# Cutting the first weight load in two and reordering the loads and scans of the second pair in a fused scan and feed-forward kernel

## Chip, core and metric

The kernel runs on one core of a Trainium2 chip. The metric is device time in microseconds (us), as the median over runs. An execution that was also profiled gives the trace; its own time and its span, from the first to the last profiled instruction, are given below.

## What is computed

A chunked state-space layer is followed by a bilinear feed-forward layer. Batch is 4, heads 8, sequence 768, head width 32, state width 16; the feed-forward layer goes from 256 to 1536 and back.

```python
# per chunk: decay L from a, intra-chunk part, carried state
M = einsum('bhin,bhjn->bhij', Cc, Bc) * L          # causal
y = einsum('bhij,bhjd->bhid', M, xc) + einsum('bhin,bhnd->bhid', Cc, state) * decay_to_i
state = decay_full * state + sum_j(B x decay)
# then, on tokens x (3072, 256)
out = ((x @ w_a) * (x @ w_b)) @ w_out
```

All inputs and the output are float32.

## The kernel before

The sequence is cut into six blocks of 128 positions. A *pair* is one block of two of the four batches, so there are twelve pairs; pairs 0 and 1 are block 0. The instruction order on each engine is written out by hand (`manual_schedule`), so what stands earlier in the program is issued earlier on its engine. Engines meet through semaphores alone.

What happens to a pair: its inputs B (`bn`), C (`cn`) and x (`xn`) are loaded in two halves each, one batch a half (`load1(queue, pair, which, bt)`, line L138, `which` being 0 for B, 1 for C and 2 for x). B and C are scaled by decay factors (`scale_bc`, L271, results `bm` and `cm`). TensorE transposes both (`transposes`, L293); ScalarE (L304) and VectorE (L305) copy the transposes out as `bt` and `ct`. TensorE makes the scores (`scores`, L327); they are masked in four pieces, three by VectorE (L361) and one by ScalarE and GpSimd (`by_pool`, copy L358 and product L359, tile `t`). x is scaled to f16 by ScalarE (`scale_x`, L255, tile `x`). Then TensorE forms the output (`pv`, `pv_u`, L370) and the state's summand (`ds_mm`, L387), and the result is copied out to `X2T` (L419, L420; for pair 0 L475 and L477). From there the feed-forward products start: `unit_mm` (L528) makes two of the twelve 128-column groups of `x @ w_a` (`aps`) or `x @ w_b` (`bps`); ScalarE copies `aps` out (L542), VectorE multiplies (L549), and `out_mm` (L564) makes the output.

The decay factors come from six scans on VectorE (`scan(lo, hi)`, L208), one a block, each from `a_sb` and a tile of zeros. `over_mid` (L211) and `sel_over_mid` (L214) prepare the factor products `fps` (L229).

The weights are float32 in memory and f16 on the chip, so they are loaded from GpSimd's queue, which converts them: `load_w(half)` (L146) loads half the columns of `w_a` and then of `w_b`, 128 x 2 x 768 elements each. GpSimd's loads go through one queue (q0) and are moved in the order of their issue. GpSimd issues, in its own instruction stream, B and C of pair 1, the first half of the weights, both halves of x of pair 1, and then computes the masked product of pair 0 and the scaled B of pair 1.

TensorE is kept busy while it would wait by products of zeros whose results nobody reads (`warmup(n, bank, cols)`, L201). Ahead of the first feed-forward products stand two of them (L710).

```python
    transposes(1, apart=True)
    scan(5, NBLK)
    over_mid(1, NBLK)
    sel_over_mid(1, NBLK, nc.vector)
    warmup(2, tcp)
    aps = [unit_mm(0, 0, Wa), unit_mm(0, 1, Wa)]
    asb = [evac_a(aps[0])]
    scores(1)
```

Later in the program the first load on SyncE's queue for pair 3 waits for the second half of `w_b` to land.

Of the kernel before, what the change touches and what calls it, by code (L numbers as in the profile page):

```python
# [10 lines left out]
f16 = mybir.dt.float16  # L11
# [16 lines left out]
def kernel(  # L28
# [13 lines left out]
    nc = tc.nc  # L42
# [4 lines left out]
    NBLK = S // Q  # L47
# [34 lines left out]
    big = ctx.enter_context(tc.tile_pool(name="big", bufs=1))  # L82
    a_sb = big.tile([BH, NBLK, Q], f32, name="a_sb")
    zero = big.tile([BH, Q], f32, name="zero")
    KC = d_ff // 2
    Wa = [big.tile([128, 2, KC], f16, name=f"Wa{t}") for t in range(2)]
    Wb = [big.tile([128, 2, KC], f16, name=f"Wb{t}") for t in range(2)]
    Wo = big.tile([128, NK, d_model], f16, name="Wo")
    X2T = big.tile([128, P0, 2, 2, Q], f16, name="X2T")
# [35 lines left out]
    def bank(name):  # L125
        return psf.tile([128, 512], f32, name=name, tag=f"ff{next(banks)}")
# [8 lines left out]
    def load1(eng, p, which, bt, i0=0, n=64):  # L135
        blk, bp = divmod(p, NBP)
        src = (B, C, x)[which][2 * bp + bt, :, blk * Q + 2 * i0 : blk * Q + 2 * i0 + 2 * n, :]
        return eng.dma_start(  # L138
            pair_in[p][which][64 * bt + i0 : 64 * bt + i0 + n].rearrange("i h r n -> i h (r n)"),
            src.rearrange("h (i r) n -> i h (r n)", r=2),  # L140
        )

    def load_w(half):
        c = slice(half * KC, (half + 1) * KC)
        return [
            nc.gpsimd.dma_start(W[half], src.rearrange("(f p) e -> p f e", p=128)[:, :, c])  # L146
            for W, src in ((Wa, moe_w_a), (Wb, moe_w_b))
        ]

    def load_wo(half):  # L150
        nc.gpsimd.dma_start(
# [35 lines left out]
    for bt in range(2):  # L187
        v = causal[64 * bt : 64 * bt + 64]
# [3 lines left out]
    load1(nc.gpsimd, 1, 0, 1)  # L192
    load1(nc.gpsimd, 1, 1, 0)
    load1(nc.gpsimd, 1, 1, 1)
    load_w(0)
    for bt in range(2):
        load1(nc.gpsimd, 1, 2, bt)

    def warmup(n, bank, cols=512):
        for _ in range(n):  # L200
            nc.tensor.matmul(  # L201
                bank[:, 0:cols], warm[:, 0:128], warm[:, 0:cols], start=True, stop=True, skip_group_check=True
            )


    def scan(lo, hi):
        for k in range(lo, hi):
            nc.vector.tensor_tensor_scan(Pr[:, k], a_sb[:, k], zero, 1.0, ALU.mult, ALU.add)  # L208
# [12 lines left out]
    def factors_mm(lo, hi, fps=None, k0=0):  # L221
        if fps is None:
            fps = bank("fps")
        w = 2 * NBP * H
        F = fps[:, k0 * w : (k0 + hi - lo) * w].rearrange("p (k r c) -> p k r c", k=hi - lo, r=2)
        for k in range(lo, hi):
            for r in range(2):
                for bt in range(2):
                    nc.tensor.matmul(  # L229
                        F[64 * bt : 64 * bt + 64, k - lo, r],  # L230
                        Pr[:, k].rearrange("p (i r) -> p r i", r=2)[:, r],
                        selr[:, k, bt],
                        start=True,
                        stop=True,
                        skip_group_check=True,
                        tile_position=(0, 64 * bt),
                    )
        return F.rearrange("p k r c -> p (k r c)")
# [5 lines left out]
    def flat(f, lo, hi):  # L244
        return f[:, lo:hi].rearrange("p k r b h -> p (k r b h)")
# [13 lines left out]
    def scale_bc(p, which, eng, factor=None):  # L259
        blk, bp = divmod(p, NBP)  # L260
        name, f = (("bm", fB), ("cm", fC))[which]
        if p >= P0 and which:
            eng.tensor_tensor(
                out=planes[p % 2][:, 4:6].rearrange("p r (h n) -> p r h n", n=N),
                in0=pair_in[p][which].rearrange("p h r n -> p r h n"),
                in1=f[:, blk, :, bp].unsqueeze(3).broadcast_to((128, 2, H, N)),
                op=ALU.mult,
            )
            return
        m_ = mid.tile([128, 2, H, N], f16, name=name, tag=name)  # L270
        eng.tensor_tensor(  # L271
            out=m_,
            in0=pair_in[p][which].rearrange("p h r n -> p r h n"),
            in1=(f[:, blk, :, bp] if factor is None else factor).unsqueeze(3).broadcast_to((128, 2, H, N)),
            op=ALU.mult,
        )
        st.setdefault(p, {})[name] = m_
        if p >= P0:
            dst = planes[p % 2][:, 0:4].rearrange("p (r e) (m f n) -> p r e m f n", e=2, f=2, n=N)
            for e in range(2):  # L280
                eng.tensor_copy(dst[:, :, e, :, e], m_.rearrange("p r (m f) n -> p r m f n", f=2)[:, :, :, e])
# [81 lines left out]
    def pv_u(p, u, py, first):  # L363
        s = st[p]
        for r in range(2):
            for g in range(4):
                for bt in range(2):
                    h = u * 4 + g
                    k = slice(64 * bt, 64 * bt + 64)
                    nc.tensor.matmul(  # L370
                        py[bt, u][32 * (g ^ 2 * bt) : 32 * (g ^ 2 * bt) + 32] if p >= P0 else py[bt][32 * g : 32 * g + 32, u * Q : (u + 1) * Q],
                        s["X16"][k, h, r, :],
                        s["T1"][k, h, r, :],
                        start=(first and u == 0 and r == 0),
                        stop=(r == 1),
                        skip_group_check=True,
                        tile_position=(64 * bt, 32 * (g ^ 2 * bt) if p >= P0 else 32 * g),
                    )
# [93 lines left out]
    def evac0(u, bt, eng, py):  # L472
        o_, i_ = X2T[:, 0, bt, u], py[bt][:, u * Q : (u + 1) * Q]
        if eng is nc.scalar:
            nc.scalar.activation(out=o_, in_=i_, func=AF.Copy, scale=YS / XS)  # L475
        else:
            nc.vector.tensor_scalar(o_, i_, YS / XS, None, ALU.mult)  # L477
# [45 lines left out]
    def unit_mm(p, k2, W):  # L523
        ps = bank("aps" if W is Wa else "bps")
        for kk in range(2):
            k = 2 * k2 + kk
            for f in range(2):
                nc.tensor.matmul(  # L528
                    ps[:, kk * 2 * Q : (kk + 1) * 2 * Q],
                    W[k // 6][:, f, k % 6 // 3 * 384 : (k % 6 // 3 + 1) * 384].rearrange("p (c kk) -> p kk c", kk=3)[  # L530
                        :, k % 3
                    ],
                    X2T[:, p, :, f],
                    start=(f == 0),
                    stop=(f == 1),
                    skip_group_check=True,
                )
        return ps

    def evac_a(a_ps, on_dve=False):  # L540
        asb = ffh.tile([128, 512], f32, name="asb", tag="asb")
        (nc.vector.tensor_copy if on_dve else nc.scalar.copy)(asb, a_ps)  # L542
        return asb
# [42 lines left out]
    def bunit(blk, k):  # L586
        s = st.setdefault(("FF", blk), {})
        if "hk" not in s:
            s["hk"] = hkb.tile([128, NK, 2 * NBP * Q], f16, name="hkb", tag="hkb")
        ps = []  # L590
        for W in (Wa, Wb):
            t_ = bank("aps" if W is Wa else "bps")
            for f in range(2):
                nc.tensor.matmul(  # L594
                    t_,
                    W[k // 6][:, f, k % 6 // 3 * 384 : (k % 6 // 3 + 1) * 384].rearrange("p (c kk) -> p kk c", kk=3)[
                        :, k % 3
                    ],
                    XB[:, blk - P0 // NBP, f].rearrange("p t j q -> p (t j q)"),
                    start=(f == 0),  # L600
                    stop=(f == 1),
                    skip_group_check=True,
                )
            ps.append(t_)
        asb = evac_a(ps[0])
        return lambda: nc.vector.tensor_tensor(out=s["hk"][:, k], in0=ps[1], in1=asb, op=ALU.mult)  # L606
# [64 lines left out]
    v = factors_mm(0, 1)  # L671
# [2 lines left out]
    warmup(1, SC[3], 128)  # L674
    scale_bc(0, 0, nc.vector)
    scale_bc(0, 1, nc.vector, v.rearrange("p (r b h) -> p r b h", r=2, b=NBP)[:, :, 0])
    tb, tcp = bank("tb"), bank("tc")
    transposes(0, [tb, tcp], lambda: warmup(1, SC[3], 128))
    nc.scalar.copy(flat(fC, 0, 1), v)
    scan(3, 4)  # L680
    warmup(1, SC[3])
    warmup(2, SC[3], 128)
    scores(0)
# [4 lines left out]
    mask(product0(1, 0))  # L688
    warmup(5, tcp)
    scale_bc(1, 1, nc.vector)  # L690
    scale_bc(1, 0, nc.gpsimd)
    py = [bank("py0"), bank("py1")]
    pv_u(0, 0, py, True)
    for bt in range(2):
# [3 lines left out]
    pv_u(0, 1, py, True)  # L698
    for bt in range(2):
        evac0(1, bt, (nc.scalar, nc.vector)[bt], py)  # L700
    scan(4, 5)
    w1 = load_w(1)
    for bt in range(2):
        load1(nc.gpsimd, 2, 0, bt)
    warmup(1, tcp, 128)
    transposes(1, apart=True)
    scan(5, NBLK)
    over_mid(1, NBLK)
    sel_over_mid(1, NBLK, nc.vector)
    warmup(2, tcp)  # L710
    aps = [unit_mm(0, 0, Wa), unit_mm(0, 1, Wa)]
    asb = [evac_a(aps[0])]
    scores(1)
# [267 lines left out]
```

## Time and profile before

| What | Value |
|---|---|
| median of 5 runs | 125.78 us (125.61 to 126.6) |
| the profiled execution's own time | 125.61 us |
| its span | 123.9 us |
| TensorE (PE) busy | 118.8 us, 96% of the span |
| VectorE (DVE) busy | 85.4 us, 69% |
| ScalarE (ACT) busy | 72.0 us, 58% |
| GpSimd (POOL) busy | 65.8 us, 53% |
| granted TensorE clock | full in all 40 slices |
| HBM read, written | 11.13 MB, 3.15 MB |

PEld is TensorE's weight load, which runs beside its products. SP is SyncE. In the profile the time from the start of the span stands first in a timeline or a chain, then the duration, both in us; a bracket at the end of a line tells how long the engine stood idle before it and what ended that. "us to landing" counts from a load's issue until its data is there. A line such as `bps<-X2T,Wb` names the tile written and the tiles read. The lines L... are those of the kernel before. Ends of TensorE's products are modelled, and spans on POOL are rough.

### The profile page before, as it was taken

To read this page: it belongs to the slowest core of one execution; us is meant where nothing else is said; L and a number is where in the kernel's file an instruction comes from. 1 tells how busy PE (TensorE), PEld (TensorE's weight loads), DVE (VectorE), ACT (ScalarE), POOL (GpSimd) and SP (SyncE) were. 2 spreads that over 40 slices of the span, in tenths; PEclk is the share of its full clock that TensorE was granted. 3 is DMA by queue.
4 is the path that set the end of the run, shared out by engine and by line. 5 is a ranking of instruction groups with operands and counts; after the bars stand their busy time and mean duration, and the time that the engine had idled before them with its cause. 6 is when DMAs were issued, how large, how long until landed. Compare 5 with 4: busy or idle time off the path is not lost.

```text
span 123.9 us, 4408 instructions
## 1 busy us (share of the span) xinstructions
PE 118.8 (96%) x1775; PEld 81.5 (66%) x1775; DVE 85.4 (69%) x162; ACT 72.0 (58%) x142; POOL 65.8 (53%) x112
## 2 busy tenths in 40 slices
PE   5889999999999999999999999999999999999990
PEld 2436789978898888744467465757464775555890
DVE  1786896795967678498964989748889544747200
ACT  0466755766364785887548746474637746657220
POOL 7999996999987497099930868039400000000000
PEclk9999999999999999999999999999999999999999
DMA  3999999997689569988364351658431023010132
GB/s 65 168 166 233 170 214 155 196 161 145 89 208 135 84 176 109 154 147 222 59 119 98 85 84 32 105 104 153 108 70 42 0 47 85 1 24 19 27 106 85
DMA packets 41844, 13.78 MB, mean 111 GB/s; under 512 B 36592, under 2 KB 41360, under 8 KB 41824
## 3 DMA queue, kind: packets, MB, share of 16 engines
q1 hardware_dynamic: 37408, 8.94, 41.5%
q0 software_dynamic: 2336, 4.13, 17.8%
q10 hardware_dynamic: 2080, 0.43, 1.8%
q8 instruction: 14, 0.23, 0.9%
q14 instruction: 6, 0.05, 0.1%
HBM read 11.13 MB, written 3.15 MB: 115 GB/s over the span
## 4 chain that ended last, share of the span: by engine, by line
PE 88%; POOL 7%; issue 1%; DVE 1%; ACT 1%; POOLq 0%; ACTq 0%
PE ops L622 17%; PE aps L594 17%; PE bps L594 16%; PE aps L528 9%; PE ops L564 9%; PE bps L528 9%; PE SC L327 3%; PE SC L370 3%; PE fps L229 1%; POOL xn L138 1%; POOL cn L138 1%; PE SC L387 1%; PE SC L435 1%; POOL bm L271 1%; PE SC L293 1%
## 5 line engine op out<-in xcount | busy, mean ns | idle before, releaser
L542 ACT COPY asb<-aps 128x512 f32<-128x512 f32 x72 | 41.8, 587 | 14.2 <-PE aps L594 9.5
L606 DVE TENSOR_TENSOR hkb<-bps,asb 128x512 f16<-128x512 f32 x48 | 32.3, 688 | 12.9 <-ACT asb L542 12.0
L594 PE MATMUL aps<-XB,Wa 128*128 128x512 f16 x96 | 28.6, 379 | 0.1
L594 PE MATMUL bps<-XB,Wb 128*128 128x512 f16 x96 | 28.6, 379 | 0.0
L622 PE MATMUL ops<-Wo,hkb 128*128 128x256 f16 (+1 forms) x204 | 22.5, 267 | 0.0
L622 PEld LDWEIGHTS <-hkb 128*128 128x128 f16 x204 | 18.5, 98 | 3.0
L361 DVE TENSOR_TENSOR t<-SC,causal_ri 128x512 f16<-128x512 f32 x26 | 16.6, 682 | 4.7 <-PE SC L327 4.7
L549 DVE TENSOR_TENSOR hk<-bps,asb 128x512 f16<-128x512 f32 x24 | 16.1, 683 | 3.7 <-ACT asb L542 3.2
L594 PEld LDWEIGHTS <-Wb 128*128 128x128 f16 x96 | 9.9, 103 | 11.1 <-issue 0.4
L594 PEld LDWEIGHTS <-Wa 128*128 128x128 f16 x96 | 9.7, 103 | 9.3 <-issue 0.7
L528 PE MATMUL aps<-X2T,Wa 128*128 128x256 f16 x96 | 14.3, 273 | 0.1
L634 ACT ACTIVATE osb<-ops 128x256 f32<-128x256 f32 (+1 forms) x16 | 6.0, 376 | 14.2 <-PE ops L622 14.1
L528 PE MATMUL bps<-X2T,Wb 128*128 128x256 f16 x96 | 14.1, 273 | 0.0
L359 POOL TENSOR_TENSOR t<-tmp,causal_ri 128x512 f16<-128x512 f32 x6 | 6.9, 1158 | 11.8 <-ACT tmp L358 11.7
L564 PE MATMUL ops<-Wo,hk 128*128 128x256 f16 x96 | 11.6, 273 | 0.0
L257 POOL TENSOR_SCALAR x<-xn 128x512 f16<-128x512 f32 x7 | 10.4, 1490 | 0.6
L528 PEld LDWEIGHTS <-Wa 128*128 128x128 f16 x96 | 9.4, 103 | 1.4 <-DVE X2T L420 0.2
L528 PEld LDWEIGHTS <-Wb 128*128 128x128 f16 x96 | 9.8, 103 | 0.7
L564 PEld LDWEIGHTS <-hk 128*128 128x128 f16 x96 | 8.9, 98 | 1.5 <-DVE hk L549 0.2
L361 DVE TENSOR_TENSOR t<-SC,causal 128x512 f16<-128x512 f32 x13 | 8.2, 683 | 0.9 <-PE SC L327 0.8
L271 POOL TENSOR_TENSOR bm<-bn,fB 128x256 f16<-128x256 f32 x11 | 7.1, 643 | 2.9 <-PE SC L327 1.9
L465 ACT ACTIVATE XB<-SC 64x512 f16<-64x512 f32 (+1 forms) x9 | 5.3, 593 | 4.0 <-PE SC L387 3.7
(86 smaller groups left out, 122.3 us busy)
## 6 DMA issues: line engine op xcount, KB each, us to landing
xn<-in_x_dram SPq DMA_DIRECT2D x13, 128.0 KB, 3.6
out_dram<-osb SPq DMA_DIRECT2D x24, 64.0 KB, 2.0
out_dram<-osb SPq DMA_DIRECT2D x11, 128.0 KB, 3.3
bn<-in_B_dram SPq DMA_DIRECT2D x20, 64.0 KB, 2.9
xn<-in_x_dram POOLq DMA_DIRECT2D x10, 128.0 KB, 4.1
cn<-in_C_dram SPq DMA_DIRECT2D x18, 64.0 KB, 3.3
Wa<-in_moe_w_a_dram POOLq DMA_DIRECT2D x2, 384.0 KB, 5.8
Wb<-in_moe_w_b_dram POOLq DMA_DIRECT2D x2, 384.0 KB, 7.2
```

Of the source, the lines that this page charges most:

```text
L257: eng.tensor_scalar(xo, xi, XS, None, ALU.mult)
L271: eng.tensor_tensor(out=m_, in0=pair_in[p][which].rearrange("p h r n -> p r h n"), in1=(f[:, blk, :, bp] if factor is None else factor).un ...
L359: nc.gpsimd.tensor_tensor(out=o_, in0=tmp, in1=c_, op=ALU.mult)
L361: nc.vector.tensor_tensor(out=o_, in0=i_, in1=c_, op=ALU.mult)
L528: nc.tensor.matmul(ps[:, kk * 2 * Q : (kk + 1) * 2 * Q], W[k // 6][:, f, k % 6 // 3 * 384 : (k % 6 // 3 + 1) * 384].rearrange("p (c kk) -> ...
L542: (nc.vector.tensor_copy if on_dve else nc.scalar.copy)(asb, a_ps)
L549: nc.vector.tensor_tensor(out=s["hk"][:, 2 * k2 : 2 * k2 + 2, :].rearrange("p k q -> p (k q)"), in0=b_ps, in1=asb, op=ALU.mult)
L564: nc.tensor.matmul(o_ps[:, 0:d_model], hk[:, k, bt * Q : (bt + 1) * Q], Wo[:, k, :], start=(k == 0), stop=(k == NK - 1), skip_group_check= ...
L594: nc.tensor.matmul(t_, W[k // 6][:, f, k % 6 // 3 * 384 : (k % 6 // 3 + 1) * 384].rearrange("p (c kk) -> p kk c", kk=3)[:, k % 3], XB[:, b ...
L606: return lambda: nc.vector.tensor_tensor(out=s["hk"][:, k], in0=ps[1], in1=asb, op=ALU.mult)
L622: nc.tensor.matmul(o_ps[:, 0:w], hk[:, k, c * Q : (c + 1) * Q], Wo[:, k, cs], start=(k == 0), stop=(k == NK - 1), skip_group_check=True,)
L634: nc.scalar.activation(out=o_sb[:, 0:w], in_=o_ps[:, 0:w], func=AF.Copy, scale=1.0 / (YS * YS))
```

## The change

The first half of `w_a` becomes two tiles of 128 x 2 x 384, each with a load of its own; `up_columns` picks the right tile for a group of columns. GpSimd's issue order for the first loads becomes: B and C of pair 1 as before, the two pieces of `w_a`, the first half of x of pair 1, the first half of `w_b`. The second half of x of pair 1 is issued later, after GpSimd has scaled B of pair 1, and ahead of the second half of the weights. The scans of blocks 3, 4 and 5 are issued sooner on VectorE: the fourth scan ahead of the copy of pair 0's transposed C, the fifth ahead of the masked products of pair 0, the sixth after the scaled C of pair 1 and ahead of the last output copy of pair 0. The two zero products ahead of the first feed-forward products are taken out.

```diff
-    Wa = [big.tile([128, 2, KC], f16, name=f"Wa{t}") for t in range(2)]
+    Wa0 = [big.tile([128, 2, KC // 2], f16, name=f"Wa0{g}") for g in range(2)]
+    Wa = [None, big.tile([128, 2, KC], f16, name="Wa1")]
...
+    def load_part(t, src, c0):
+        c = slice(c0, c0 + t.shape[2])
+        return nc.gpsimd.dma_start(t, src.rearrange("(f p) e -> p f e", p=128)[:, :, c])
+
+    def up_columns(W, k, f):
+        t, g = W[k // 6], k % 6 // 3
+        v = Wa0[g][:, f] if W is Wa and k < 6 else t[:, f, g * 384 : (g + 1) * 384]
+        return v.rearrange("p (c kk) -> p kk c", kk=3)[:, k % 3]
...
     load1(nc.gpsimd, 1, 1, 1)
-    load_w(0)
-    for bt in range(2):
-        load1(nc.gpsimd, 1, 2, bt)
+    load_part(Wa0[0], moe_w_a, 0)
+    load_part(Wa0[1], moe_w_a, KC // 2)
+    load1(nc.gpsimd, 1, 2, 0)
+    load_part(Wb[0], moe_w_b, 0)
...
     scale_bc(0, 1, nc.vector, v.rearrange("p (r b h) -> p r b h", r=2, b=NBP)[:, :, 0])
+    scan(3, 4)
     tb, tcp = bank("tb"), bank("tc")
     transposes(0, [tb, tcp], lambda: warmup(1, SC[3], 128))
     nc.scalar.copy(flat(fC, 0, 1), v)
-    scan(3, 4)
+    scan(4, 5)
...
     scale_bc(1, 1, nc.vector)
+    scan(5, NBLK)
     scale_bc(1, 0, nc.gpsimd)
+    load1(nc.gpsimd, 1, 2, 1)
...
-    scan(4, 5)
-    w1 = load_w(1)
+    w1 = [load_part(Wa[1], moe_w_a, KC), load_part(Wb[1], moe_w_b, KC)]
     for bt in range(2):
         load1(nc.gpsimd, 2, 0, bt)
     warmup(1, tcp, 128)
     transposes(1, apart=True)
-    scan(5, NBLK)
     over_mid(1, NBLK)
     sel_over_mid(1, NBLK, nc.vector)
-    warmup(2, tcp)
     aps = [unit_mm(0, 0, Wa), unit_mm(0, 1, Wa)]
```

More of the change, by code (lines that the diff above doesn't have):

```diff
@@ L141, in load1 @@
         )
[L143 to L148, printed above, removed]
+    def load_part(t, src, c0):
[5 more added lines that the diff above has]
+        return v.rearrange("p (c kk) -> p kk c", kk=3)[:, k % 3]
     def load_wo(half):
@@ L529, in unit_mm @@
                     ps[:, kk * 2 * Q : (kk + 1) * 2 * Q],
-                    W[k // 6][:, f, k % 6 // 3 * 384 : (k % 6 // 3 + 1) * 384].rearrange("p (c kk) -> p kk c", kk=3)[
-                        :, k % 3
-                    ],
+                    up_columns(W, k, f),
                     X2T[:, p, :, f],
@@ L595, in bunit @@
                     t_,
-                    W[k // 6][:, f, k % 6 // 3 * 384 : (k % 6 // 3 + 1) * 384].rearrange("p (c kk) -> p kk c", kk=3)[
-                        :, k % 3
-                    ],
+                    up_columns(W, k, f),
                     XB[:, blk - P0 // NBP, f].rearrange("p t j q -> p (t j q)"),
```

## The prediction

> **What bounds the kernel now.** I read the page's busy shares first, then its chain of what ended last, then that chain in order of time around the change.
>
> ```profile
> PE 118.8 (96%) x1775; PEld 81.5 (66%) x1775; DVE 85.4 (69%) x162; ACT 72.0 (58%) x142; POOL 65.8 (53%) x112
> ```
> ```profile
> 9.23 0.86 POOL bm L271
> 10.09 0.05 issue
> 10.13 0.40 PE SC L293 x4
> 10.53 0.43 PE tc L201 x2
> 10.96 0.87 PE aps L528 x8
> 11.84 0.36 PE SC L327 x32
> 12.20 0.55 PE aps L528 x4
> 12.74 0.59 PE fps L229 x16
> 13.33 1.42 PE bps L528 x12
> 14.76 0.43 PE SC L370 x32
> ```
>
> TensorE is busy nearly throughout, and from 15.69 us on the chain is TensorE alone, product behind product. So whatever delays or advances its first products of pair 1 moves the end by as much. Before 10.13 us the chain runs over POOL's loads and its scaled B; then TensorE runs through to `pv` of pair 1 (L370). The two zero products stand in it with 0.43 us. The question is whether something else already stands ready to take their place. The timeline of weight loads, then of ScalarE, shows `pv`'s start:
>
> ```profile
> 14.68 0.24 PEld L370 LDWEIGHTS <-x 64*32 64x32 f16 x32 [0.21 <-ACT x L255]
> ```
> ```profile
> 13.76 0.24 ACT L242 COPY fC<-fps 128x64 f32<-128x64 f32 x1
> 13.94 0.63 ACT L255 ACTIVATE x<-xn 128x512 f16<-128x512 f32 x1
> ```
>
> `pv` waited for ScalarE's scaled x, which started at 13.94 and ended at 14.57. Its inputs' landing is read from the list of loads, asked in four narrow windows so that each answer holds one load (`w_a`, `w_b`, two halves of x, issued at 5.09, 5.82, 6.54 and 7.23):
>
> ```profile
> Wa<-in_moe_w_a_dram POOLq DMA_DIRECT2D x1, 384.0 KB, 5.4
> ...
> Wb<-in_moe_w_b_dram POOLq DMA_DIRECT2D x1, 384.0 KB, 6.8
> ...
> xn<-in_x_dram POOLq DMA_DIRECT2D x1, 128.0 KB, 6.7
> ...
> xn<-in_x_dram POOLq DMA_DIRECT2D x1, 128.0 KB, 6.6
> ```
>
> They land at 10.5, 12.6, 13.2 and 13.8. The last one is 0.1 before ScalarE's start: the data of x sets `pv`'s start in the kernel before, within 0.1 us.
>
> **Zero products.** Two go: -0.43 us at 10.53. The first feed-forward products need piece one of `w_a` at 10.5 and piece two (column group 3) at about 11.0. All of `w_a` landed at 10.5; piece one should come about 0.8 sooner, so both are there. The scores (L327) need ScalarE's second `bt` copy, which ends at 11.41, so 0.35 of the 0.43 is left there: `w_b` would be wanted at 13.33 - 0.35 = 12.98.
>
> **x ahead of `w_b`.** One queue moves these loads in order, so `w_b` lands when the first half of x did, at 13.2 instead of 12.6. `bps` then starts at 13.3 to 13.4, where it started before (13.26 in the timeline, 13.33 in the chain). The 0.35 turns into a wait for `w_b`, 0 to +0.1 against before.
>
> **Second half of x later.** It is issued at 10.03 to 10.75 instead of 7.23 to 7.99, but its turn in the queue is behind `w_b`, at about 13.2, and the bytes ahead of it are the same: it lands at 13.8 as before. ScalarE starts at 13.94, `pv` at 14.69. Nothing here gains.
>
> **Two pieces.** The rows read shrink from 3072 bytes to 1536, 16 more rows on each of 16 engines. Queue rows of the windows 8 to 11 and 5.5 to 6 us (packets, MB, share of 16 engines):
>
> ```profile
> q0 software_dynamic: 397, 0.58, 114.3%
> ...
> q10 hardware_dynamic: 350, 0.09, 80.0%
> ```
>
> A weight row takes 1.143 x 16 x 3000 / 397 = 138 ns, a 256-byte row of x 0.80 x 16 x 500 / 350 = 18 ns. A straight line through both gives 73 ns at 1536 bytes, so two cost 7 ns more than one: 16 x 7 = 0.11 us. Bounds: 0, and 16 x 138 = 2.2 us if a half row cost a whole one. I take 0.1, as short rows are shown to be cheap. This lies on the path, since x and `w_b` come behind.
>
> The Trainium skill speaks against the split ("DMA: Bandwidth & Descriptors", Measured and Anatomy of one DMA): each transfer has a fixed cost of about 2.0 us beside its bytes. By that the sum would be +2.0 us if transfers stood one behind another; this trace has the two halves of x landing 0.6 us apart, fixed cost included.
>
> **POOL's order.** Ahead of its first mask POOL issues seven loads, as before, at 0.69 to 0.76 each whether 64 or 384 KB (POOL timeline): no change there, ±0.05. After the scaled B comes one issue more, 0.72:
>
> ```profile
> 9.23 0.85 POOL L271 TENSOR_TENSOR bm<-bn,fB 128x256 f16<-128x256 f32 x1
> 10.03 0.74 POOL L146 DMA_DIRECT2D Wa<-in_moe_w_a_dram  x1
> 10.77 0.74 POOL L146 DMA_DIRECT2D Wb<-in_moe_w_b_dram  x1
> 11.48 1.43 POOL L138 DMA_DIRECT2D bn<-in_B_dram  x2
> 12.99 1.16 POOL L359 TENSOR_TENSOR t<-tmp,causal 128x512 f16<-128x512 f32 x1
> ```
>
> The mask of pair 1 moves from 12.99 to 13.71 and ends at 14.87. The second half of `pv` reads it, from about 14.81: 0.06 to 0.1 late, hidden as far as `pv` itself is late. Behind it two loads of C, `Wo`, and the small products up to `hsx` end at 18.05 instead of 17.33, and TensorE takes that at 18.42: covered by 0.37. The next scaled C (21.35) stood 1.08 idle for its load, which takes up the 0.72. The second weights land at 16.1 and 18.4, wanted after 19.5: the later issue is hidden by the backlog, and +0.1 by 1.5 us of slack; SP, whose pair 3 loads wait for the latter, shifts by the same 0.1.
>
> **Scans.** Moved, three of 0.40 us. The first fills 0.38 of idle before 6.32, the second the first's old place. VectorE drops 0.8 us between 10.26 and 11.35, where nobody on the path waited: the masks stood idle for the scores. The third now starts at about 9.53, while POOL scales B. The only row of such a meeting is the scaled B itself: its line in the tile's answer has 616/621/852 ns as least, median and most, and the 852 is this one, beside VectorE's scaled C (9.18 to 9.60), which also reads SBUF alone. So a meeting costs POOL 0.23. The third scan can find POOL at work since about 9.46 and stand behind it, which costs `X2T` (10.05) up to 0.4 and the path nothing, or go first and hold POOL by up to 0.40. I take the first, since POOL has by then waited longest: 0 on the path.
>
> The Trainium skill's rule ("SBUF — State Buffer", SBUF: two separate sides) is that a VectorE operation with two SBUF inputs and a GpSimd operation that reads SBUF lock each other out for a whole instruction. It agrees in kind with the 0.23, and by it the meeting costs one side a full instruction, so the sum would be +0.4 if the scan wins.
>
> **Sum.** Zero products -0.43, given back +0.35 to `w_b` and the rest to x; pieces +0.1; POOL's mask hidden in that; scans 0. `pv` starts 0.1 later: 125.61 becomes 125.7 in the profiled execution. The median stood 0.17 above it: 125.9. A measurement of this kernel can tell about 0.5%, or 0.63 us, from no change.
>
> **The rivals.** *The gain is kept* (0.10): the queue runs faster and `w_b` and x come 0.3 or more sooner. For it: landings vary. Against it: the engines of the queue are busy at over 100% from 8 to 11 us, and no bytes are saved. All 0.43 kept gives 125.35, and 0.2 more at the copy to `X2T` 125.15.
>
> *The scan holds POOL* (0.15): the scaled B ends at 10.48, the second half of x and the mask follow, the mask ends at 15.27, `pv` waits 0.4: 126.2 to 126.3, still within 0.63.
>
> *The pieces are dear* (0.30), the rival on the other side: half rows cost more than the line says, at the queue between 7 and 14 us, and all of it shows in x's landing. Price 0.1 to 2.2; over 0.63 from 40 ns a row more. At 40 to 80 ns it is 0.6 to 1.3: 126.5 to 127.1; at the bound 128.0. Against it: the 256-byte rows. For it: no row of half this size was converted to f16 on the way.
>
> *It doesn't do what it says*: if piece one came after 10.9, the place of the zero products would be idle time and nothing else would change; the time is the forecast's.
>
> **Numbers.** Forecast 0.45 (125.6 to 126.2), the others as given. The range, 125.3 to 127.1, leaves out half of the kept gain and the dear pieces above 80 ns. Faster by over 0.5% only with more than the zero products: 0.08. Slower by over 0.5% is most of the dear pieces: 0.30. Within: 0.62.
>
> **What would show it.** In the profile after: `aps` at 10.4 to 10.7, then an idle stretch of about 0.3 before `bps`, ended by `w_b`; ScalarE's scale of x at 13.9 to 14.1, and `pv` at 14.7 to 14.9, ended by x or POOL's `t`. The scaled B on POOL at 0.85 us as now says that the scan stood behind, 1.2 us that it went first. I am wrong if x lands before 13.5 or `pv` starts before 14.4.

## The result and the profile after

The changed kernel takes 126.66 us (median of 36 runs, 125.84 to 128.32); the kernel before takes 125.99 us over 62 runs beside it. The ratio is 1.0047, with a 95% interval of 1.0032 to 1.0063: about 0.6 us slower, just inside the 0.5% that the prediction called no change, and inside its range. The forecast of 125.9 us, 0.1 above the kernel before, was too low. Ratios, here and below, compare the runs within 1.5% of their kernel's fastest run; slower ones, most of them at a lower granted clock, are left out of them.

The profiled execution of the changed kernel took 127.56 us by itself, 1.95 more than that of the kernel before. It is one of the slower runs of this kernel. It shows where time can go; the size is read from the medians.

First the busy shares and the chain's shares on the page of the changed kernel:

```profile
PE 119.2 (95%) x1773; PEld 81.4 (65%) x1773; DVE 85.5 (68%) x162; ACT 71.9 (57%) x142; POOL 66.2 (53%) x113
...
PE 89%; DMA 5%; POOL 1%; ACT 1%; DVE 1%; issue 1%; ACTq 0%; POOLq 0%
```

The chain's shares on the page of the kernel before:

```profile
PE 88%; POOL 7%; issue 1%; DVE 1%; ACT 1%; POOLq 0%; ACTq 0%
```

TensorE's busy time is nearly as before (118.8), and a load now carries 5% of the chain, which before held no load. Next the chain in order of time, between 9 and 18.5 us:

```profile
9.28 0.56 POOL bm L275
9.84 5.88 DMA xn<-in_x_dram
...
15.80 0.64 ACT x L259
...
16.49 0.50 PE SC L374 x32
...
17.01 0.44 DVE X2T L424
...
17.49 0.62 PE aps L532 x4
```

Before, TensorE's own products filled the chain from 10.13 to `pv` at 14.76. Now the chain leaves POOL's scaled B at 9.84 for the second half of x and comes back only when that load has landed, at 15.72. `pv` (L374) starts at 16.49 instead of 14.76, and the next feed-forward products at 17.49 instead of 15.69. The shift of 1.8 is never made up.

The timelines of TensorE's products, of its weight loads and of ScalarE (start, duration, then in brackets the idle time before and what ended it) show the waits themselves:

```profile
10.36 1.33 PE L532 MATMUL aps<-X2T,Wa 128*128 128x256 f16 x8
...
13.93 1.49 PE L532 MATMUL bps<-X2T,Wb 128*128 128x256 f16 x12 [0.74 <-DMA Wb<-in_moe_w_b_dram]
```
```profile
16.48 0.24 PEld L374 LDWEIGHTS <-x 64*32 64x32 f16 x32 [1.34 <-ACT x L259]
```
```profile
13.62 0.24 ACT L246 COPY fC<-fps 128x64 f32<-128x64 f32 x1
15.80 0.63 ACT L259 ACTIVATE x<-xn 128x512 f16<-128x512 f32 x1 [1.95 <-DMA xn<-in_x_dram]
```

`aps` starts at 10.36, the zero products gone and piece one there. Then TensorE waits 0.74 for `w_b`, and later over 1 us for x, because ScalarE stood idle 1.95 for the load. The list of loads, in two narrow windows, gives the two that matter (issued at 7.23 and 9.84; the last figure is us from issue to landing):

```profile
Wb<-in_moe_w_b_dram POOLq DMA_DIRECT2D x1, 384.0 KB, 6.7
```
```profile
xn<-in_x_dram POOLq DMA_DIRECT2D x1, 128.0 KB, 5.9
```

`w_b` landed at 13.9, where the prediction had 13.2, and the second half of x at 15.7, where it had 13.8.

In the traces every load steps its semaphore sixteen times, which is read here as one step for each of the 16 DMA engines when its share is done; what waits for the load starts after the sixteenth (ScalarE at 15.80, after the step at 15.72). The steps in the trace, in the order of time (us from the span's start):

| load | kernel | issued | mean of 8th and 9th engine | 15th | 16th |
|---|---|---|---|---|---|
| `w_b` | before | 5.82 | 12.1 | 12.35 | 12.64 |
| `w_b` | after | 7.23 | 12.5 | 12.94 | 13.88 |
| x, second half | before | 7.23 | 13.45 | 13.64 | 13.85 |
| x, second half | after | 9.84 | 13.24 | 13.65 | 15.72 |

On fifteen engines the second half of x lands when it did before, within 0.01 us, or sooner. On one it is 2 us late, and that one counts.

### The profile page after: what moved, and what is told of

Read it like the earlier page. It is cut to its first block, busy times and chain, and to the rows that moved or that the text cites. A ratio compares the mean times of both kernels' runs of the same rounds, so it can differ in the third digit from the quotient of the medians.

```text
span 125.8 us, 4404 instructions
## 1 busy us (share of the span) xinstructions
PE 119.2 (95%) x1773; PEld 81.4 (65%) x1773; DVE 85.5 (68%) x162; ACT 71.9 (57%) x142; POOL 66.2 (53%) x113
## 4 chain that ended last, share of the span: by engine, by line
PE 89%; DMA 5%; POOL 1%; ACT 1%; DVE 1%; issue 1%; ACTq 0%; POOLq 0%
PE ops L622 17%; PE aps L596 17%; PE bps L596 17%; PE ops L566 9%; PE aps L532 8%; PE bps L532 7%; DMA xn<-in_x_dram 5%; PE SC L331 3%; PE SC L205 3%; PE SC L374 3%; PE fps L233 1%; PE SC L391 1%; POOL t L363 1%; PE SC L439 1%; ACT x L259 1%
## 5 line engine op out<-in xcount | busy, mean ns | idle before, releaser
L544 ACT COPY asb<-aps 128x512 f32<-128x512 f32 x72 | 41.9, 586 | 14.1 <-PE aps L596 9.1
L622 PEld LDWEIGHTS <-hkb 128*128 128x128 f16 x204 | 18.5, 98 | 3.0
L551 DVE TENSOR_TENSOR hk<-bps,asb 128x512 f16<-128x512 f32 x24 | 16.2, 683 | 4.2 <-ACT asb L544 3.2
L532 PE MATMUL bps<-X2T,Wb 128*128 128x256 f16 x96 | 14.1, 273 | 0.7 <-DMA Wb<-in_moe_w_b_dram 0.7
L634 ACT ACTIVATE osb<-ops 128x256 f32<-128x256 f32 (+1 forms) x16 | 6.0, 376 | 14.3 <-PE ops L622 14.2
L363 POOL TENSOR_TENSOR t<-tmp,causal_ri 128x512 f16<-128x512 f32 x6 | 6.9, 1158 | 11.8 <-ACT tmp L362 11.7
L261 POOL TENSOR_SCALAR x<-xn 128x512 f16<-128x512 f32 x7 | 10.4, 1489 | 1.7 <-DMA xn<-in_x_dram 1.2
```

Of the source, the lines that this page charges most:

```text
L261: eng.tensor_scalar(xo, xi, XS, None, ALU.mult)
L363: nc.gpsimd.tensor_tensor(out=o_, in0=tmp, in1=c_, op=ALU.mult)
L532: nc.tensor.matmul(ps[:, kk * 2 * Q : (kk + 1) * 2 * Q], up_columns(W, k, f), X2T[:, p, :, f], start=(f == 0), stop=(f == 1), skip_group_c ...
L551: nc.vector.tensor_tensor(out=s["hk"][:, 2 * k2 : 2 * k2 + 2, :].rearrange("p k q -> p (k q)"), in0=b_ps, in1=asb, op=ALU.mult)
L622: nc.tensor.matmul(o_ps[:, 0:w], hk[:, k, c * Q : (c + 1) * Q], Wo[:, k, cs], start=(k == 0), stop=(k == NK - 1), skip_group_check=True,)
L634: nc.scalar.activation(out=o_sb[:, 0:w], in_=o_ps[:, 0:w], func=AF.Copy, scale=1.0 / (YS * YS))
```

## Experiments

The first theory was *late issue*: the second half of x, issued at about 10 us instead of 7.2, is late on the slowest engines, and that is the whole loss. The rivals: the order of the loads, the pieces, POOL's shifted work, or the moved scans cost it. All ratios are against runs of the kernel before on the same chip, with 95% intervals. Some of the edits below are written short, with a comment in place of the lines.

**Late issue alone (late_x).** The kernel before, with only this step of the change:

```diff
-    for bt in range(2):
-        load1(nc.gpsimd, 1, 2, bt)
+    load1(nc.gpsimd, 1, 2, 0)
...
     scale_bc(1, 0, nc.gpsimd)
+    load1(nc.gpsimd, 1, 2, 1)
```

> The kernel before with one part of the change: the second half of x of pair 1 is issued after the scaled B instead of ahead of POOL's first mask; nothing is split, reordered or removed. Theory 'late issue' (the loads issued late are caught by the slowest of the 16 engines of the queue): +0.4 to +0.7 us against before. Theory 'order' (w_b behind a half of x): 0. Theory 'pieces' (half rows are dear): 0. Theory of the prediction (bytes ahead of x are the same, so its landing is): 0, within 0.2.

126.78 us against 126.08; ratio 1.0057 (1.0031 to 1.0082). This step alone costs what the whole change costs. In its profiled execution the granted clock was 0.84 of full between 9 and 20 us, and a load of pair 0 came late. The second half of x landed at 14.96 there, but ScalarE was still at other work, so this trace doesn't show the wait; the time carries the verdict.

**Order alone (swap_x).** The kernel before with the first half of x ahead of `w_b`, everything issued early:

```diff
-    load_w(0)
-    for bt in range(2):
-        load1(nc.gpsimd, 1, 2, bt)
+    # Wa whole, x first half, Wb whole, x second half
```

> The kernel before with one part of the change: the first half of x of pair 1 goes ahead of w_b in the queue, the second half stays right behind w_b, all issued early; zero products, scans and the whole load of w_a stay. Theory 'order': +0.4 to +0.7 us, since w_b lands with the former first half of x and bps waits. Prediction: w_b lands 0.6 later, wanted at 13.3 and there at 13.2, so 0 to +0.1. Theories 'late issue' and 'pieces': 0.

126.16 us; ratio 1.001 (0.9984 to 1.0035). The order costs nothing that shows. `w_b` landed at 13.58 and the second half of x at 13.82.

**`w_b` ahead of x (after_wb_first).** The changed kernel with these two loads the other way round:

```diff
     load_part(Wa0[1], moe_w_a, KC // 2)
-    load1(nc.gpsimd, 1, 2, 0)
     load_part(Wb[0], moe_w_b, 0)
+    load1(nc.gpsimd, 1, 2, 0)
```

> The changed kernel with w_b back ahead of the first half of x; pieces, late second half, scans and removed zero products stay. Theory 'order': bps no longer waits, the time falls to before's or 0.1 under it. Theory 'late issue': x sets the start of pv as in the changed kernel, +0.4 to +0.7 us against before. Theory 'pieces': the same +0.4 to +0.7.

127.59 us; ratio 1.0124 (1.0082 to 1.0167), from 6 runs. It makes it worse. ScalarE's timeline shows the same wait as in the changed kernel, here with both halves of x late (14.95 and 15.44):

```profile
15.53 0.63 ACT L259 ACTIVATE x<-xn 128x512 f16<-128x512 f32 x1 [1.70 <-DMA xn<-in_x_dram]
```

Why it costs more than the changed kernel is not explained: in its profile `pv` starts at 16.21, no later than in the changed kernel's.

**Scans where they were (after_scans_back).**

```diff
-    scan(3, 4)      # ahead of the copy of pair 0's C
-    scan(4, 5)      # ahead of pair 0's masked products
-    scan(5, NBLK)   # after the scaled C of pair 1
+    # all three where the kernel before has them
```

> The changed kernel with the scans of blocks 3 to 5 where they were. Theory 'scans' (the meeting of scan and POOL costs the path): back to before's time, within 0.2. The others: like the changed kernel, +0.4 to +0.7 us against before, since the copy to X2T that the scan holds up is followed by the wait for w_b anyway.

126.95 us; ratio 1.0067 (1.0034 to 1.01). The loss stays, so the scans are not its cause. In its chain `w_b` came last and x just after (14.42 and 14.97):

```profile
7.25 7.17 DMA Wb<-in_moe_w_b_dram
...
14.47 1.49 PE bps L532 x12
15.96 0.43 PE SC L374 x32
```

**Late issue and pieces undone (after_early).** The moved scans stay, the zero products stay out, the first half of x stays ahead of `w_b`; `w_a` is whole again and the second half of x is issued early, behind `w_b`:

```diff
-    load_part(Wa0[0], moe_w_a, 0)
-    load_part(Wa0[1], moe_w_a, KC // 2)
-    load1(nc.gpsimd, 1, 2, 0)
-    load_part(Wb[0], moe_w_b, 0)
+    load_w(0)                       # Wa, x first half, Wb
+    load1(nc.gpsimd, 1, 2, 1)
...
     scale_bc(1, 0, nc.gpsimd)
-    load1(nc.gpsimd, 1, 2, 1)
```

> The changed kernel without its pieces and without the late issue: w_a whole, then the first half of x, w_b, and the second half of x right behind it, all issued ahead of POOL's first mask; scans moved and the two zero products removed. Theory 'late issue': within 0.2 us of before, x landing on all engines by 14.0. Theory 'zero products' (their removal or the scans cost): +0.5. Theory that the removed 0.43 can be kept: -0.3 to -0.4.

126.1 us against 126.33; ratio 0.999 (0.9961 to 1.0018). The loss is gone. The chain runs through TensorE again, from `w_a` on:

```profile
5.13 5.71 DMA Wa<-in_moe_w_a_dram
...
10.88 1.06 PE aps L529 x8
...
13.44 1.43 PE bps L529 x12
14.86 0.43 PE SC L371 x32
```

`pv` starts at 14.86, against 14.76 before. With the zero products out, the scans moved and the loads early, the time is that of the kernel before; its interval reaches down to -0.5 us, so a small gain isn't excluded by the time alone. In the profile the place of the zero products went to a wait for `w_a`, which landed at 10.84 here:

```profile
10.88 1.06 PE L529 MATMUL aps<-X2T,Wa 128*128 128x256 f16 x8 [0.35 <-DMA Wa<-in_moe_w_a_dram]
```

**POOL's shift alone (pool_issue).** The kernel before, with a spare load of 5 KB issued where the change puts the second half of x, so that all of POOL's later work moves by one issue:

```diff
     scale_bc(1, 0, nc.gpsimd)
+    nc.gpsimd.dma_start(spare, ph_t.ap())
```

> The kernel before with one small load more on POOL, of 5 KB into a spare tile, issued after the scaled B: every step of POOL from there moves by one issue (0.7 us) as in the changed kernel, but x is issued early. Theory 'landing' (the late issue costs through x's landing): within 0.2 us of before, x landing by 14.0. Theory 'POOL shift' (it costs through the mask and the steps behind it): +0.3 to +0.7, pv's second half waiting for POOL's t.

126.33 us against 126.33; ratio 1.0023 (0.9986 to 1.0059). The mask of pair 1 starts at 13.44 and ends at 14.67, and `pv` starts at 14.75 as before: hidden in the profile, though the interval leaves room for up to 0.7 us. The spare load itself, 5 KB, landed at 14.72, with its middle engines at 13.3.

**Late issue with pieces, `w_b` first (late_split).** The kernel before with the second half of x late and `w_a` in two pieces, without the change's order, scans or missing zero products:

```diff
-    load_w(0)
-    for bt in range(2):
-        load1(nc.gpsimd, 1, 2, bt)
+    load_part(Wa0[0], moe_w_a, 0)
+    load_part(Wa0[1], moe_w_a, KC // 2)
+    load_part(Wb[0], moe_w_b, 0)
+    load1(nc.gpsimd, 1, 2, 0)
...
     scale_bc(1, 0, nc.gpsimd)
+    load1(nc.gpsimd, 1, 2, 1)
```

> The kernel before with the second half of x issued late and w_a in two pieces; order, scans and zero products as before. Against the run with the late issue alone (+0.7 us): theory 'late issue' with cheap pieces: +0.7 to +0.9. Theory 'pieces': +1.3 or more.

127.21 us against 126.33; ratio 1.0075 (1.0045 to 1.0104). Late issue alone gave 1.0057: the intervals overlap, so a price of the pieces beside it is not resolved. The second half of x landed at 15.34.

**The load early, on SyncE's queue (after_x1_sp).** The changed kernel with the second half of x issued at 5.2 on another queue:

```diff
+    load1(nc.sync, 1, 2, 1)         # with SyncE's first loads
...
     scale_bc(1, 0, nc.gpsimd)
-    load1(nc.gpsimd, 1, 2, 1)
```

> The changed kernel with the second half of x issued early from SyncE's queue, which is idle then, instead of late from POOL's. Theory 'late issue': x lands well before 13, pv is no longer ended by x; w_b, which shares the engines with it, lands near 13.9 and sets bps: +0.3 to +0.7 against before. Theory that a late engine delays whatever is loaded: the same. Better than before only if w_b lands by 13.0: -0.3.

126.89 us against 126.33; ratio 1.0053 (1.0022 to 1.0085). x was no longer waited for (landed 10.39), but the second piece of `w_a` was, so what the profile shows is a loss of another kind:

```profile
5.82 5.69 DMA Wa<-in_moe_w_a_dram
11.51 0.05 issue
11.55 0.40 PE aps L533 x2
```

SyncE's queue wasn't idle, as the expectation had it: half of B, issued there at 3.87, landed at 8.54. `pv` started at 15.05, 0.29 later than in the kernel before; the ratio stands for 0.7, and where the rest arises is not shown.

**A copy issued late (dup_x_late).** The late load may be late itself, or its arrival may disturb the loads ahead of it. The kernel before, all its loads early, plus 128 KB of x into a spare tile, issued late:

```diff
     scale_bc(1, 0, nc.gpsimd)
+    nc.gpsimd.dma_start(spare[64:128], x[3, :, 0:Q, :])   # same shape and size
```

> The kernel before, x issued early as there, with the second half of x of pair 1 loaded once more, late, into a spare tile that nobody reads, at the place where the changed kernel issues it (128 KB more). Theory 'waiting load' (a load that is issued late is itself late on the slowest engine, the loads ahead of it are not): x and w_b land as before, by 14.0 and 12.8, the spare copy at 15 or later, time within 0.2 us of before. Theory 'disturbance' (issuing it slows the engines at what they are moving): w_b and the early x land 0.5 to 1.5 later too, time +0.4 to +0.8.

126.31 us against 126.2; ratio 1.0032 (1.0007 to 1.0057). The list of loads, for the spare copy issued at 10.09:

```profile
spare<-in_x_dram POOLq DMA_DIRECT2D x1, 128.0 KB, 5.8
```

It landed at 15.86, as the late x did, its 8th engine at 14.40. `w_b` landed at 12.63, as before. The early second half of x landed at 14.16, 0.3 later than before, but on all engines alike: 0.44 lay between the mean of its 8th and 9th engine and the last, against 0.41 before. So the tail is the late load's own, and those ahead of it don't share it. The time settles less: 1.0032 is about 0.4 us, more than the one theory allowed and at the lower edge of the other.

**Pieces with everything early (after_early_split).** The changed kernel with the second half of x issued behind `w_b`, and half of B of pair 1 moved to SyncE's queue:

```diff
+    load1(nc.sync, 1, 0, 1)
...
-    load1(nc.gpsimd, 1, 0, 1)
...
     load_part(Wb[0], moe_w_b, 0)
+    load1(nc.gpsimd, 1, 2, 1)
...
     scale_bc(1, 0, nc.gpsimd)
-    load1(nc.gpsimd, 1, 2, 1)
```

> The changed kernel with one part undone: the second half of x is issued right behind w_b, ahead of POOL's first mask. So that POOL still issues seven loads there, one half of B of pair 1 goes to SyncE's queue. Theory 'late issue': x lands by 14.0 and the time is before's, within 0.2 us, pieces, order, scans and zero products notwithstanding. Theory 'pieces': +0.4 or more against before.

Ratio 1.0068 (1.0013 to 1.0123), from only 4 runs. The second half of x landed at 13.96 with the pieces in place (8th engine 13.38), without the tail; the granted clock of this profiled execution was 0.84 between 9 and 20 us. But the moved half of B came at 10.72 and POOL waited for it, so the time does not tell the price of the pieces:

```profile
10.88 0.62 POOL L276 TENSOR_TENSOR bm<-bn,fB 128x256 f16<-128x256 f32 x1 [1.62 <-DMA bn<-in_B_dram]
```

**The change once more (after_again).** The same kernel, to see whether the 2 us on the slowest engine come again.

> The changed kernel as it is, for a second profile. Theory 'late issue': +0.5 to +0.7 us against before, the second half of x landing at 14.7 to 15.7 on the slowest engine and setting pv's start. Theory that the first profile was an odd one: x by 14.0, pv by 14.9.

126.67 us against 126.2; ratio 1.0063 (1.0031 to 1.0095). They do, on two engines now (15.92 and 16.15), later still than the 15.7 that was expected. From the chain:

```profile
10.18 5.97 DMA xn<-in_x_dram
...
16.24 0.64 ACT x L259
...
16.92 0.50 PE SC L374 x32
```

**The load late, on ScalarE's queue (after_x1_act).** Is it late because it stands behind the weights in GpSimd's queue?

```diff
         evac0(0, bt, nc.scalar, py)
+    load1(nc.scalar, 1, 2, 1)
...
     scale_bc(1, 0, nc.gpsimd)
-    load1(nc.gpsimd, 1, 2, 1)
```

> The changed kernel, with the second half of x of pair 1 issued at about the same late moment (about 9.6 us), but on ScalarE's own queue and not behind the weights on GpSimd's. Theory that the load is late because it waits in GpSimd's queue behind w_b: on another queue it lands within about 3 us, before 13.0, ScalarE's scaled x no longer waits for it and starts at 13.6 to 14.0, pv at 14.7 to 15.1, and the time is that of the kernel before, ratio 0.996 to 1.002 (w_b, sharing the engines with it, lands no later than 13.9; ScalarE loses up to 0.4 us on its X2T copy, off the path). Rival, that any load issued this late lands on the slowest engine 1 to 2 us later, whatever its queue: it lands after 14.5, pv starts after 15.5, ratio 1.004 to 1.007.

127.54 us against 126.17; ratio 1.0103 (1.0053 to 1.0154), from 6 runs. My theory falls: issued at 9.38 on its own queue, the load landed at 15.74. The loss is larger than the rival's 1.004 to 1.007, too; why is not shown. This queue moves x in rows of 256 bytes, 512 of them, which have records of their own (queue q10; the columns are packets, MB, share of 16 engines). The windows 11.7 to 12.7 and 13.7 to 15.7 us:

```profile
q0 software_dynamic: 97, 0.13, 75.2%
q10 hardware_dynamic: 378, 0.09, 43.2%
```
```profile
q0 software_dynamic: 273, 0.40, 111.9%
q10 hardware_dynamic: 36, 0.01, 3.0%
```

Some three quarters of x moved in one microsecond. The last 36 packets took 1.6 us, though each takes only 0.030 x 16 x 2000 / 36 = 27 ns. The start times of these last rows stand in series, of which the last one is 14.08, 14.22, 14.36, 14.51, 14.65, 14.79, 14.93, 15.08, 15.22. That is one row of x in 0.14 us, and a weight row was worked out as 138 ns. So on the engines that are behind, one row of x goes for one row of weights, and the weights are by then those of the next load, the second half of `w_a`, issued at 10.06 (`w_b` had landed at 13.55). For this queue that shows what drew the tail out; why these engines were behind it does not show.

## Why the prediction was right, and which term was mis-sized

*What bounds the kernel.* Right. TensorE's first products of pair 1 moved, and the end moved by as much: 1.73 at `pv`, 1.95 at the end of the profiled execution.

*Zero products.* Right. `aps` came at 10.36 (forecast 10.4 to 10.7), and the place went to a wait for `w_b`. The wait was 0.74, not 0.3.

*x ahead of `w_b`.* Right in kind, and costless alone (1.001). But `w_b` was put at 13.2 and came at 13.88 and 13.74 in the two profiles of the changed kernel. The slowest engines make the difference: for `w_b`, 1.0 to 2.0 lay between the mean of the 8th and 9th engine and the last in all seven profiles with the second half of x issued late, 0.5 to 0.8 in all seven with it issued early, those of the kernel before and of the spare copy among them.

*Second half of x later.* This is the term that was mis-sized: 0 in the sum, about 0.7 us in the times (late issue alone 1.0057; undone together with the pieces 0.999), and 1.9 at x's landing in the profiled execution. The step that failed is "its turn in the queue is behind `w_b`, at about 13.2, and the bytes ahead of it are the same: it lands at 13.8 as before". The middle engines bear it out (13.24 against 13.45). But a load has landed only with its slowest engine, and of the slowest engines nothing was said. Over the profiles:

| second half of x issued | landed |
|---|---|
| early, behind all or most of the first weights (before, swap_x, after_early, pool_issue, dup_x_late, after_early_split) | 13.5 to 14.2 |
| at 9.4 to 10.2 (late_x, changed kernel twice, after_wb_first, after_scans_back, late_split, after_x1_act) | 15.0 to 16.2 |

The starts of single packets in the traces tell what the last engine did in the changed kernel's first profile. Its two rows of x start at 14.28 and 14.71, one straight behind the other, when all the other rows had started by 12.61. Just before stands a fetch of instructions, one packet of 16 KB on queue q8, from 13.13 to 14.29 (queue row of the window 13.1 to 14.3, 0.060 x 16 x 1200 = 1150 ns):

```profile
q8 instruction: 1, 0.02, 6.0%
```

The trace doesn't name engines, so that it is the same one is inferred from the times. They meet alike in after_wb_first, late_split and dup_x_late: fetches end at 13.80, 13.85 and 14.44, and rows of the late load start at 13.79, 13.83 and 14.42 on what is the last engine. In the kernel before, such a fetch (12.44 to 13.82) held no row of x back: the last one started at 12.63. So part of the price is probably that a load issued late stands behind this fetch. It isn't all: in after_again the fetch ended at 12.63, and the last rows of x started at 15.29 and 15.55.

The prediction named "x lands before 13.5" as what would prove it wrong, and looked only to that side. Its own signs on the other side, ScalarE's scale of x at 13.9 to 14.1 and `pv` at 14.7 to 14.9, failed: 15.80 and 16.49.

*Two pieces.* The term was 0.1, from 73 ns for a half row. In the window 8.5 to 8.95 us of the changed kernel nearly all packets are half rows:

```profile
q0 software_dynamic: 122, 0.09, 137.1%
```

1.371 x 16 x 450 / 122 = 81 ns. Two cost 162 against 138, and 16 x 24 = 0.38 us, not 0.11; under the 40 ns a row that the rival needed for 0.63 us. The straight line went through a row of another queue, which isn't converted on the way; whether that is why it missed is not shown. What of the 0.38 reaches the end is not resolved: x is later still. The Trainium skill's fixed cost of 2.0 us per transfer ("DMA: Bandwidth & Descriptors", Anatomy of one DMA) doesn't add up behind one another here: the pieces landed 1.0 us apart, at 10.25 and 11.24.

*POOL's order.* Right: the mask started at 13.38 and was long done when `pv` started, and the shift alone gave 1.0023 with an interval that holds 1.

*Scans.* Right that the path pays nothing (the loss stays with the scans moved back, 1.0067). Who meets whom differed between the two profiles of the changed kernel. In after_again it went as forecast: VectorE's scaled C came first, POOL's scaled B took 0.85, and the scan stood behind it, with 0.83 instead of 0.40:

```profile
9.35 0.41 DVE L275 TENSOR_TENSOR cm<-cn,fC 128x256 f16<-128x256 f32 x1
9.68 0.83 DVE L212 TENSOR_TENSOR_SCAN Pr<-a_sb,zero 32x128 f32<-32x128 f32 x1
```
```profile
9.39 0.85 POOL L275 TENSOR_TENSOR bm<-bn,fB 128x256 f16<-128x256 f32 x1
```

In the first profile C landed later, POOL started first, its scaled B took 0.61, neither the 0.85 nor the 1.2 that were named, and VectorE's scaled C stood behind it:

```profile
9.28 0.61 POOL L275 TENSOR_TENSOR bm<-bn,fB 128x256 f16<-128x256 f32 x1
```
```profile
9.57 0.60 DVE L275 TENSOR_TENSOR cm<-cn,fC 128x256 f16<-128x256 f32 x1 [0.26 <-DMA cn<-in_C_dram]
10.10 0.41 DVE L212 TENSOR_TENSOR_SCAN Pr<-a_sb,zero 32x128 f32<-32x128 f32 x1
10.44 0.25 DVE L481 TENSOR_SCALAR X2T<-py 128x128 f16<-128x128 f32 x1
```

That is 0.60 instead of the 0.42 of the kernel before, then the scan; `X2T` came at 10.44 instead of 10.05 in both profiles, as bounded.

*The rivals.* None is shown to have happened. The loss has the sign of the dear pieces, but the late issue alone brings as much, and no rival covered a load that comes later by being issued later. That the time still fell inside the range is in part luck: the range reached above 126.2 us for the sake of the dear pieces, and 1.0047 lies just under the 0.5% that was called no change.

*Still open.* Why one to three engines fall behind at all, and why `w_b`, issued as early as ever, comes late on them when nothing of x stands behind it in the queue. The alternation with the next weights is shown for ScalarE's queue alone; on the last engine of the changed kernel's first profile the two rows of x followed each other without it.

## What to carry to other kernels

A load's landing is set by its slowest engine, so "the same bytes are ahead of it" does not say that it may be issued later: here that cost 0.7 us of 126. Look at the spread over the engines, and at what else can get in between, another queue's rows or a fetch of instructions. A shift that the chain shows with one load in it is tested most cheaply by that load's issue alone. When a wait is freed by removing filler work, name the next input in line and the spread of its landing, not only its middle.

## What the hardware showed beyond expectation

A load issued late came late on its slowest engines in both sizes and on both queues that were tried: 5 KB issued at 10.02 landed at 14.72, 128 KB issued at 10.09 at 15.86, both on GpSimd's queue, and 128 KB issued at 9.38 on ScalarE's at 15.74. In each case the 8th of the 16 engines was done by 14.4 at the latest.

Between two queues the engines that were behind gave turns row by row: one 256-byte row in 0.14 us, the time of one weight row. The Trainium skill ("DMA: Bandwidth & Descriptors", Queues, rings and completion order) has each engine take turns between queues packet by packet, some 9 to 17 descriptors at a time. The turns are seen here, and in the series above a turn is one row. Elsewhere in that trace up to 17 rows of x follow each other 0.014 us apart (from 13.55), and it doesn't tell whether weights stood waiting then.

The same page (Latency and other measured facts) reports that engines 7 and 15 are usually slower, and guesses at the fetching of GpSimd's descriptors. One to three stragglers of 16 would go with that, but no run here tells which engines they were.
